# An HGRN2 attention block with a routed feed-forward: stores of x rows half a step later, the first slots' fetch two stages earlier, the first expert's transposes three stages later

## The chip, the cores and the metric

The kernel runs on one core of a Trainium2 chip, in one launch. The metric is the device time of that core in microseconds (us). TensorE (PE) does the matrix products and transposes; VectorE (DVE), ScalarE (ACT) and GpSimd (POOL) do elementwise work; SyncE (SP) only issues transfers (DMAs). GpSimd issues DMAs too, those that gather or scatter rows by a list. Each engine takes its instructions in the order in which the program lists them.

## What is computed

```python
# attention: q, k, v, f_logit are (4, 8, 768, 48)
f = 1.0 / (1.0 + np.exp(-f_logit))
for t in range(S):
    state = f[:, :, t, :, None] * state + np.einsum('bhd,bhe->bhde', k[:, :, t], v[:, :, t])
    y[:, :, t] = np.einsum('bhd,bhde->bhe', q[:, :, t], state)
x = y.transpose(0, 2, 1, 3).reshape(3072, 384)
# router: two of eight experts for each row
noisy = x @ w_gate + np.log1p(np.exp(x @ w_noise)) * noise
top2 = np.argpartition(-noisy, 2, axis=1)[:, :2]          # weights: softmax over the two
# experts: w1 is (8, 384, 1024), w2 is (8, 1024, 384)
out[mask] += top2_w[mask, k, None] * (np.maximum(x[mask] @ w1[e], 0.0) @ w2[e])
```

## The kernel before

**Attention in 24 pieces.** The sequence is cut into six chunks of 128 tokens, for each of four batch rows: 24 pieces, `n` = 0 to 23 (`NS`). For a piece there are seven stages: `forget` (transposes and log of the forget gate), `summed` (a running sum), `decays` (exponentials), `scaled` (transposes and scaling of q and k), `scores` (the 128 x 128 score blocks, L573, multiplied by the causal mask into `A`, L576), `output` (the y products, L591 and L602, and the new state) and `features` (L626: the x rows and the router's logits in one product; ACT copies the x rows to `xs`, L631). The main loop (L1292) runs steps `i`; in step `i` the stages are called in the fixed order forget, scaled, scores, summed, output, decays, features, each for the piece `i - lag` (lags in L1293). So in the last steps step 23 does sc 23, y 22 and xp 21, step 24 does y 23 and xp 22, and step 25 does xp 23. In the text "sc 23" stands for the scores of piece 23, and so on.

**What a stage has hung on it.** After a stage is called, the loop issues loads of later pieces on SP's queue (f after `forget`, q and k after `scaled`, v after `scores`), parts of the first experts' weights, clears of the output (`zeros`, L1253, 192 KB each), a step of the router's generator (`route`), at most one put of an entry into the expert lists (`put`, L703, a GpSimd DMA), a step of `first_loads`, and, once that has set `done["turned"]`, a piece of the expert work. One such round is what the change counts as a stage. The stores of x rows (`x_rows`, a tensor in the chip's main memory) are not issued where they are made: `features` puts them into the list `xw` (L632), and the loop takes them out.

**The expert work.** After half of the chunks are routed, the first 256 rows of the first four experts' lists are taken from the rows known so far. The 24 groups of 256 list entries are called pairs; the first four are items 0 to 3 (`NE` = 4). For each pair: `fetch` (L808) loads its list entries (`slots`) on SP, `gather` (L819) gathers the x rows by them with two GpSimd DMAs of 128 rows each, `turned` (L855) transposes the 128 rows on TensorE and DVE copies them to `xt_a`, `first_layer` (L907, four blocks of two: `hp`) does the first product with a ReLU on ACT, and `second_layer` (L1014) does the second product in seven products of half size (Strassen-Winograd), for which DVE makes sums of weights (`second_sums`, L879) and of hidden values (`inner_sums`, L996). The results are scattered with addition into the output (L1023). `ahead(1, k + NR + 1)` (L914) loads the first-layer weights of a later item into the buffer that the current one has just read for the last time.

**The seam.** `first_loads` is a generator that is stepped once a stage. It waits until the puts of the first half are issued, then some stages, and then goes through a written list of fetches, gathers and the first pair's two transposes with a number of stages to pause after each. Puts are held back between the first fetch and the first gather (L1332). The weights of pair 1 (`w1[1]` L834, `w2[1]` L837, in quarters) are loaded at the end of the loop. All this order is kept as traced on every engine (`in_order`, L1393). On SP's queue each DMA also waits for the eighth one before it, since their completion semaphores are taken in turn.

Of the kernel before, what the change touches and what calls it, by code (L numbers as in the profile page):

```python
# [331 lines left out]
def kernel(  # L332
# [157 lines left out]
    def load_router(part):  # L490

        if part < 2:
            for i, w in ((part, (moe_w_gate, moe_w_noise)[part]),):
                for odd in range(2):
                    for par in range(2):
                        nc.gpsimd.dma_start(out=w_rt[par * DP:par * DP + D, odd::2, XW + i * E:XW + (i + 1) * E],
                                          in_=w.rearrange("(a o r d) e -> o r d a e", o=2, r=2, d=D)[odd, par ^ odd])
        else:
            c = part - 2
            nc.sync.dma_start(out=noise[:, c], in_=moe_noise.rearrange("(b s) e -> s b e", b=B)[c * C:(c + 1) * C])  # L500
# [8 lines left out]
    xw, puts, n_put = [], [], []  # L509
# [8 lines left out]
    def load(nm, n):  # L518
        c, b = n // B, n % B
        if n < NCH * B:  # L520
            nc.sync.dma_start(out=pads[nm][n % RING[nm]][:, :, 0:D],
                              in_={"f": f_logit, "q": q, "k": k, "v": v}[nm][b, :, c * C:(c + 1) * C, :].rearrange("h t d -> t h d"))

    def clamp(n, engine=nc.gpsimd):
        if n < NCH * B:
            raw = pads["f"][n % RING["f"]][:, :, 0:D]
            engine.tensor_scalar(raw, raw, XMIN, None, ALU.max)
# [286 lines left out]
    def gather(p, halves=(0, 1)):  # L814

        if 0 in halves:
            xg[p] = moved.tile([128, 2, DM], F32, tag="xg", name=f"xg{p}", bufs=4)
        for s in halves:
            nc.gpsimd.indirect_dma_start(out=xg[p][:, s, :], out_offset=None, in_=x_rows[0:HALF * B * C] if p < NE else x_rows,  # L819
                                         in_offset=bass.IndirectOffsetOnAxis(ap=slots[p][:, s, 0:1], axis=0))  # L820
# [10 lines left out]
    def part_of_weights(k, which, part):  # L831
        if which == 1:
            few = slice(part * FF // 4, (part + 1) * FF // 4)
            nc.sync.dma_start(out=w1[k][:, :, few], in_=moe_w1[k].rearrange("(k p) f -> p k f", p=128)[:, :, few])  # L834
        else:
            few = slice(part * FO // 4, (part + 1) * FO // 4)
            nc.sync.dma_start(out=w2[k][:, few], in_=moe_w2[k].rearrange("(f p) d -> p f d", p=128)[:, few])  # L837
# [8 lines left out]
    def turned(p, s):  # L846
        k = item_of(p)
        if k < NE:
            to = xt_a[:, :, k % 2 * 256 + s * 128:k % 2 * 256 + (s + 1) * 128]
        else:  # L850
            side, at = columns(k)[p - first_of[k]][s]
            to = (wide[0] if side else xt_a)[:, :, at:at + 128]
        xp = one_bank(f"xgp{p}_{s}")
        for i in range(KO):
            nc.tensor.transpose(xp[:, i * 128:(i + 1) * 128], xg[p][:, s, i * 128:(i + 1) * 128], ident)  # L855
        (nc.vector.tensor_copy if p < NE else nc.scalar.copy)(to, xp[:, 0:DM].rearrange("d (k t) -> d k t", k=KO))
# [3 lines left out]
    def ahead(what, until):  # L860
        if what in (1, 2):
            most = len(items) if what == 1 else done[1]
        else:
            most = min(NP if len(n_put) == NCH * B * 2 else NE, NP if what == "fetch" else done["fetch"])
        while done[what] < min(until, most):
            t = done[what]
            done[what] += 1
            fetch(t) if what == "fetch" else gather(t) if what == "gather" else weights(t, what)
# [356 lines left out]
    first = len(nc.cur_bb.bb.instructions)  # L1225
# [5 lines left out]
    def warm_up(count):  # L1231
        for _ in range(count):
            nc.tensor.matmul(warm[:, 0:128], lhsT=ones, rhs=ones, start=True, stop=True)
# [24 lines left out]
    def first_loads():  # L1258
        while n_routed < HALF or len(n_put) < HALF * B * 2:
            yield  # L1260
        for _ in range(7):
            yield
        for what, p, pause in (("fetch", 1, 4), ("first", 0, 0), ("second", 0, 3), ("fetch", 2, 7), ("turned", 0, 0),
                               ("first", 1, 3), ("second", 1, 1), ("fetch", 3, 1)):
            if what == "fetch":
                ahead(what, p)
            elif what == "first":
                gather(p, (0,))
            elif what == "second":
                gather(p, (1,))  # L1270
                done["gather"] = p + 1
            else:
                for half in range(2):
                    turned(p, half)
                    yield
                done["turned"] = True
            for _ in range(pause):
                yield

    def tables():  # L1280
        for i, val in enumerate((0, 0, FAR, 0)):
            nc.gpsimd.memset(empty[:, :, i], val)
        nc.gpsimd.memset(entry, 0)
        for i, ids in ((0, row_of), (2, token)):
            nc.gpsimd.tensor_copy(entry[:, :, :, :, i], ids.unsqueeze(3).broadcast_to((128, NCH, B, 2)))
        nc.gpsimd.memset(zero, 0.0)
# [5 lines left out]
    for i in range(-3, NS + 2):  # L1292
        order = [(forget, -3), (scaled, -1), (scores, 0), (summed, -2), (output, 1), (decays, -2), (features, 2)]  # L1293
        if i < 0:
            order[0:2] = order[1::-1]
        for stage, lag in order:
            n = i - lag
            if not 0 <= n < NS:
                continue
            stage(n)  # L1300
            if stage is forget:
                load("f", n + 4)
                if n > 1:
                    clamp(n + 2)
                if n == 5:
                    tables()
            elif stage is scaled:
                for nm in "qk":
                    load(nm, n + 2) if n < 4 else load(nm, n + 3)
                    if n == 3:  # L1310
                        load(nm, n + 3)
                if n in (1, 2):
                    load_router(n - 1)
                while xw:
                    xw.pop(0)()
            elif stage is scores:
                for m in (n + 1,) if n < 4 else (2 * n - 3, 2 * n - 2) if n < 6 else (n + 3,):
                    load("v", m)
                if n in (2, 6, 7, 8, 9, 10):
                    load_router(2 + (2, 6, 7, 8, 9, 10).index(n))  # L1320
                elif n == 5:
                    nc.sync.dma_start(out=lists.rearrange("(p r) w -> p r w", p=128), in_=empty)
            elif stage is output:
                if 9 <= n < 17:
                    part_of_weights(0, 1 + (n - 9) // 4, (n - 9) % 4)
                elif n >= NS - 2:
                    part_of_weights(1, 1, 1 + (n - NS + 2) * 2)
            elif stage is features and n >= NS - 4:
                part_of_weights(1, 1, (n - NS + 4) * 2) if n < NS - 2 else zeros(4)
            next(router, None)  # L1330
            slot += 1
            if puts and slot % (2 if n_routed == HALF else 3) == 0 and not (done["fetch"] and not done["gather"]):  # L1332
                puts.pop(0)()
            next(first_pairs, None)

            if done["turned"] and (n_first < 5 or i >= NS - 3 and stage is not forget) and (n_first < 11 or i >= NS - 1):
                next(pieces)
                n_first += 1
        if i < 0:
            warm_up(4)  # L1340
        if i >= NS - 1:
            while xw:
                xw.pop(0)()
        n = i - 2
        if n >= 0 and n % B == B - 1:
            c = n // B
            router = chain(router, route(c))
            n_routed = c + 1
            if c == HALF - 1:
                router = chain(router, enough())  # L1350
                first_pairs = first_loads()
            if c == NCH - 1:
                router = chain(router, plan(), beyond())
# [19 lines left out]
    for item, piece in pieces:  # L1373
        p = first_of[item] + max(0, piece - 8) // 7 if item >= NE else item
# [58 lines left out]
```

## Time and profile before

| what | us |
|---|---|
| median of 3 runs | 655.39 |
| lowest, highest of them | 652.59, 659.07 |
| the profiled execution, its time | 659.87 |
| the profiled execution, its span | 658.1 |
| TensorE matmuls, busy | 637.8 |
| VectorE, ScalarE, GpSimd, busy | 442.8, 254.1, 270.2 |

The span is that from the first instruction to the last on the core. The mean granted TensorE clock is 0.987 of full speed. TensorE is busy in nearly all of the span, so the place to look is not a mean over the span but the few stretches in which it is not, and what ends them: the waits of TensorE, the chain of work that ended last, and the timelines of the engines that feed it. DMAs are read by the time at which they are issued and the time at which they land: over the whole run a store of x rows lands after 4.4 us (median), a fetch of slots after 7.7, a put into the lists after 6.1, a gather after 4.6, a clear of the output after 9.6, a whole weight load of 1.5 MB after 8.5.

### The profile page before, as it was taken

The numbers are of one execution on the slowest core, as the hardware profiler recorded it, in microseconds if no ns is written. First come the engines' busy times: TensorE is split into PE (matmuls) and PEld (weight loads), VectorE is DVE, ScalarE is ACT, GpSimd is POOL, SyncE is SP. The second block draws the span as 40 slices with busy tenths as digits, with TensorE's granted clock in tenths as the row PEclk, the third lists the DMA queues.
The fourth block names the chain that finished last, engine by engine and source line by source line (L and its number), as shares of the span: only waits on it lengthen the run. The fifth ranks groups of instructions, "written<-read, shape, count | busy, mean of one in ns | idle before, by whom it ended". The sixth has DMA issues, their size and how long they took to land.

```text
span 658.1 us, 12894 instructions
## 1 busy us (share of the span) xinstructions
PE 637.8 (97%) x4883; PEld 551.1 (84%) x4883; DVE 442.8 (67%) x993; ACT 254.1 (39%) x602; POOL 270.2 (41%) x301
## 2 busy tenths in 40 slices
PE   8999999979999999999999999999999999999991
PEld 8999999868989999989758965995698579899891
DVE  6777877954566577677657575666666666766751
ACT  6876776642222133233332233223332332232320
POOL 7743999743188521252501450334035114413021
PEclk9999999998999999999999999999999999999996
DMA  9999898774799323368707560925275247602112
GB/s 191 193 220 205 181 191 173 179 209 110 256 348 237 64 36 86 82 192 286 195 28 245 98 192 0 316 41 176 74 242 127 63 143 191 178 2 26 21 25 29
DMA packets 153897, 96.31 MB, mean 146 GB/s; under 512 B 115600, under 2 KB 146320, under 8 KB 153824
## 3 DMA queue, kind: packets, MB, share of 16 engines
q1 hardware_dynamic: 141648, 76.12, 42.0%
q0 software_dynamic: 12176, 19.25, 15.0%
q8 instruction: 41, 0.67, 0.4%
q14 instruction: 32, 0.26, 0.1%
HBM read 75.97 MB, written 19.62 MB: 145 GB/s over the span
## 4 chain that ended last, share of the span: by engine, by line
PE 90%; DMA 5%; SPq 1%; DVE 1%; POOL 1%; issue 0%; ACT 0%; POOLq 0%; DVEq 0%
PE y L1014 31%; PE P L932 8%; PE W L932 5%; PE Z L932 5%; PE V L932 5%; PE X L932 5%; PE hp L907 5%; PE sc L573 4%; PE y L591 4%; PE xp L626 3%; PE xgp L855 2%; PE y L602 2%; PE kp L533 1%; PE ds L597 1%; PE fp L533 1%; PE qp L533 1%
## 5 line engine op out<-in xcount | busy, mean ns | idle before, releaser
L1023 POOL DMA_INDIRECT out_dram<-ys,slots x48 | 80.3, 1672 | 150.0 <-ACT ys L1084 121.9
L1014 PE MATMUL y<-qk_all,f_all 128*128 128x192 f32 x576 | 105.3, 327 | 0.5 <-DVE f_all L996 0.5
L1014 PEld LDWEIGHTS y<-qk_all,f_all 128*128 128x128 f32 x576 | 93.3, 190 | 1.1 <-DVE f_all L996 1.1
L819 POOL DMA_INDIRECT xg<-x_rows,slots x48 | 52.9, 1102 | 50.8 <-DMA slots<-lists 35.0
L1014 PE MATMUL y<-w,hs_b 128*128 128x192 f32 x320 | 59.1, 328 | 0.0
L703 POOL DMA_INDIRECT lists<-entry,sloti x48 | 54.8, 1142 | 10.3 <-issue 9.5
L1014 PEld LDWEIGHTS y<-w,hs_b 128*128 128x128 f32 x320 | 52.9, 190 | 0.9
L1158 POOL DMA_INDIRECT out_dram<-ys_q,slots_q x5 | 8.6, 1720 | 104.4 <-DVE ys_q L1156 104.4
L907 PE MATMUL hp<-xt_a,w 128*128 128x256 f32 x192 | 43.4, 382 | 0.0
L968 ACT ACTIVATE hs_b<-hs_b 128x256 f32<-128x256 f32 (+1 forms) x32 | 15.1, 470 | 71.7 <-DVE hs_b L948 71.7
L907 PEld LDWEIGHTS hp<-xt_a,w 128*128 128x128 f32 x192 | 35.9, 190 | 4.9 <-issue 0.3
L932 PE MATMUL X<-xt_a,w 128*128 128x256 f32 (+1 forms) x128 | 39.7, 432 | 0.0
L932 PE MATMUL Z<-xt_b,v_all 128*128 128x256 f32 (+1 forms) x128 | 39.7, 432 | 0.0
L1073 DVE TENSOR_TENSOR ys<-P,y 128x192 f32<-128x192 f32 x24 | 8.5, 354 | 41.6 <-PE y L1014 25.6
L948 DVE TENSOR_TENSOR hs_b<-hs_a,X 128x256 f32<-128x256 f32 (+1 forms) x32 | 15.6, 487 | 29.9 <-PE X L932 29.7
L576 DVE TENSOR_TENSOR A<-sc,causal 128x1024 f32<-128x1024 f32 x24 | 29.3, 1221 | 8.9 <-PE sc L573 8.8
L1014 PE MATMUL y<-w,f_all 128*128 128x192 f32 x192 | 35.2, 326 | 0.0
L1084 ACT ACTIVATE ys<-ys,slots 128x384 f32<-128x384 f32 x23 | 14.1, 615 | 54.1 <-DVE ys L1080 54.1
L932 PEld LDWEIGHTS X<-xt_a,w 128*128 128x128 f32 x128 | 24.3, 190 | 10.1
L932 PEld LDWEIGHTS Z<-xt_b,v_all 128*128 128x128 f32 x128 | 24.3, 190 | 10.1
L948 DVE TENSOR_TENSOR hs_a<-hs_a,P 128x256 f32<-128x256 f32 (+1 forms) x64 | 31.1, 486 | 1.4
L1014 PEld LDWEIGHTS y<-w,f_all 128*128 128x128 f32 x192 | 31.8, 190 | 0.0
(200 smaller groups left out, 1442.2 us busy)
## 6 DMA issues: line engine op xcount, KB each, us to landing
w<-in_moe_w_dram SPq DMA_DIRECT2D x16, 1536.0 KB, 8.5
w_q<-in_moe_w_dram SPq DMA_DIRECT2D x10, 1536.0 KB, 10.3
w<-in_moe_w_dram SPq DMA_DIRECT2D x16, 384.0 KB, 6.1
f_all<-in_f_logit_dram SPq DMA_DIRECT2D x24, 192.0 KB, 3.7
qk_all<-in_q_dram SPq DMA_DIRECT2D x24, 192.0 KB, 4.9
qk_all<-in_k_dram SPq DMA_DIRECT2D x24, 192.0 KB, 4.9
v_all<-in_v_dram SPq DMA_DIRECT2D x24, 192.0 KB, 4.4
x_rows<-xs SPq DMA_DIRECT2D x24, 192.0 KB, 4.4
```

The costliest lines, as they stand in the source:

```text
L533: nc.tensor.transpose(p[:, cols(hp)], flat[:, cols(hp)], ident)
L573: nc.tensor.matmul(sc[:, par, cols(hp)], lhsT=kQ[n][rows(par), cols(hp)], rhs=qP[n][rows(par), cols(hp)], start=True, stop=True)
L576: nc.vector.tensor_tensor(A[n].rearrange("j r (a i) -> j (r a) i", i=C), sc.rearrange("j r (a i) -> j (r a) i", i=C), causal.unsqueeze(1). ...
L591: nc.tensor.matmul(at(hp, par), lhsT=vt[:, 2 * hp + par, :], rhs=A[n][:, par, cols(hp)], start=(hp < 2), stop=(c == 0 and hp >= HP - 2))
L626: nc.tensor.matmul(xp[:, hp, :], lhsT=yT[n][:, hp % 2, cols(hp // 2)], rhs=w_rt[:, hp, :], start=True, stop=True)
L703: into = nc.gpsimd.indirect_dma_start(out=lists, out_offset=bass.IndirectOffsetOnAxis(ap=sloti[:, r, b:b + 1], axis=0), in_=entry[:, c, b, ...
L819: nc.gpsimd.indirect_dma_start(out=xg[p][:, s, :], out_offset=None, in_=x_rows[0:HALF * B * C] if p < NE else x_rows, in_offset=bass.Indir ...
L907: nc.tensor.matmul(hp[:, o, :], lhsT=w1[home(k)][:, i, (fo + o) * 128:(fo + o + 1) * 128], rhs=xt_a[:, i, k % 2 * 256:(k % 2 + 1) * 256], ...
L932: nc.tensor.matmul(to, lhsT=x, rhs=y, start=start, stop=stop)
L948: nc.vector.tensor_tensor(to, x, y, ALU.add)
L1014: nc.tensor.matmul(P[name], lhsT=x[:, o, :], rhs=y[:, o, :], start=(o == 0), stop=(o == FH - 1))
L1023: into = nc.gpsimd.indirect_dma_start(out=out, out_offset=bass.IndirectOffsetOnAxis(ap=slots[p][:, s, 2:3], axis=0), in_=ys[s], in_offset= ...
```

## The change

`first_loads` steps five stages and not seven before the first fetch, and the list after it has the first pair's transposes behind the gathers of the second pair, with other pauses. Counted in stages after the puts of the first half, the first fetch goes from 7 to 5, the first gathers from 11 to 9, the second fetch from 14 to 12, the first pair's two transposes from 21 and 22 to 24 and 25, the second pair's two gathers from 23 and 26 to 17 and 18, and the third fetch from 27 to 26. The expert pieces start after the transposes, so they too start three stages later. The stores in `xw` are taken out after `output` and no longer after `scaled`, that is three stages later in the same step.

```diff
@@ first_loads
-        for _ in range(7):
+        for _ in range(5):
             yield
-        for what, p, pause in (("fetch", 1, 4), ("first", 0, 0), ("second", 0, 3), ("fetch", 2, 7), ("turned", 0, 0),
-                               ("first", 1, 3), ("second", 1, 1), ("fetch", 3, 1)):
+        for what, p, pause in (("fetch", 1, 4), ("first", 0, 0), ("second", 0, 3), ("fetch", 2, 5), ("first", 1, 1), ("second", 1, 6),
+                               ("turned", 0, 0), ("fetch", 3, 1)):
@@ main loop, after `scaled`
                 if n in (1, 2):
                     load_router(n - 1)
-                while xw:
-                    xw.pop(0)()
@@ main loop, after `output`
             elif stage is output:
+                while xw:
+                    xw.pop(0)()
                 if 9 <= n < 17:
                     part_of_weights(0, 1 + (n - 9) // 4, (n - 9) % 4)
```

In the list, `("fetch", p, ...)` loads the slots of all pairs below `p` that are not loaded yet, `("first", p, ...)` and `("second", p, ...)` are the two gathers of pair `p`, and `("turned", 0, 0)` is the two transposes of pair 0, a stage apart.

## The prediction

> **What bounds the kernel now.** I read the page's busy shares first: PE is busy 637.8 of 658.1 us, so only 20.3 us of the span are idle TensorE time. I split these with the waits view of PE and the timeline of its ends: 1.8 us at the start, 4.16 us in one wait near 142 us, 0.46 us in one near 190 us, and 13.9 us after the last matmul (it ends at 644.2). Elsewhere TensorE runs through: one attention step, as a sum of rows of the chain (0.44 fp, 0.44 qp, 0.44 kp, 0.44 kp turned, 1.09 sc, 1.02 y, 0.47 ds, 0.60 y, 1.07 xp), is 6.01 us, and steps follow each other every 6.0 us. The stage to price is the end of attention. First the waits of PE (total us, times, longest), then its timeline there (start us, us, line, op, and the idle time before):
>
> ```profile
> PE xgp L855 <- DMA xg<-x_rows,slots: 4.2, 1, 4.2
> ```
>
> ```profile
> 138.11 1.16 PE L573 MATMUL sc<-qP,kQ 64*128 64x128 f32 x16
> 139.20 1.09 PE L591 MATMUL y<-A,v_all 128*64 128x128 f32 x16
> 140.22 0.67 PE L602 MATMUL y<-qP,st 64*64 64x128 f32 x16
> 140.82 1.15 PE L626 MATMUL xp<-w_rt,yT 128*128 128x112 f32 x8
> 146.12 0.87 PE L855 MATMUL xgp<-ident,xg 128*128 128x128 f32 x3 [4.16 <-DMA xg<-x_rows,slots]
> 146.93 2.08 PE L573 MATMUL sc<-qP,kQ 64*128 64x128 f32 x16
> 148.94 0.90 PE L855 MATMUL xgp<-ident,xg 128*128 128x128 f32 x3
> ...
> 151.67 0.94 PE L602 MATMUL y<-qP,st 64*64 64x128 f32 x16
> ```
>
> The first expert's transposes wait for gathered rows, and the last scores (L573) stand behind them though their inputs were ready at 139.7. And after the wait the same scores take 2.08 us instead of 1.16. The windows view confirms a lower clock (stretch; length, PE, PEld, DVE, ACT, POOL busy; granted clock, DMA share, GB/s):
>
> ```profile
> 130.00:140.00 10.00, 10.00 (x152) 8.84 (x150) 9.11 (x16) 6.38 (x19) 1.35 (x2) 1.00 0.74 164
> 140.00:150.00 10.00, 5.84 (x54) 4.46 (x52) 3.04 (x7) 1.14 (x4) 8.15 (x12) 0.77 0.71 206
> 150.00:160.00 10.00, 10.00 (x85) 8.43 (x87) 5.21 (x19) 2.32 (x5) 3.81 (x7) 0.89 0.39 84
> ```
>
> Third, the SP queue's timeline, because it issues the fetch, the stores and the weights:
>
> ```profile
> 134.41 0.37 SPq L521 DMA_DIRECT2D v_all<-in_v_dram  x1
> 134.87 0.84 SPq L808 DMA_DIRECT2D slots<-lists  x1
> ...
> 142.77 14.65 SPq L632 DMA_DIRECT2D x_rows<-xs  x2
> 157.47 0.43 SPq L834 DMA_DIRECT2D w<-in_moe_w_dram  x1
> ...
> 176.70 2.34 SPq L837 DMA_DIRECT2D w<-in_moe_w_dram  x4
> ```
>
> The fetch leaves at 134.87 and lands 4.37 us later (chain of waits), the gather starts at 140.06 and lands 5.93 us later, at 145.99: that releases PE. A store of x rows held SP for 14.65 us (the stall delayed its input), and the second weights of pair 1 left only at 176.70, landing at 185.97; the sums that read them (L879) waited 6.67 us, which is the 0.46 us of PE at 190.
>
> **What the Trainium skill says.** "TensorE: Matmul & The Clock Gate", What's actually happening: the array falls to half clock after an idle window of about 3.4 us and needs about as long of work to recover, and the window is free-running, so this varies by run. The trace agrees: 4.16 us of idleness, then groups at up to 1.8 times their length until about 152. "DMA: Bandwidth & Descriptors", Anatomy of one DMA: a transfer costs about 2 us fixed, and waits for semaphores are held on the issuing sequencer. The 4 KB fetch took 4.37 us here, so the fixed part is larger under this load; SP's 14.65 us shows the second point.
>
> **The change, part by part.** The durations are of the profiled execution: 658.1 us of span, 659.87 as its time, 4.5 above the median 655.39 of the three runs.
>
> *Transposes three stages back.* Nothing is added: six transposes, two DVE copies (0.56 us) and all later pieces keep their number. By the built program's order PE now does sc 23, y 22, xp 21, first transposes, y 23, second transposes, xp 22, then the four hp blocks with xp 23 after the first. From xp's end at 141.96 at full speed: sc 1.09, y 1.02+0.60, xp 1.07 end at 145.74; there the first transposes need rows that in the trace before landed at 145.99, even with no earlier fetch. Wait left: 0.25 us at most, of 4.16. Next y 23 (its A: DVE 1.22 us after sc ends at 143.05, so 144.4; its v load needs to land before 146.1) ends at 147.69; the second transposes need the second gather, issued 1.34 us behind the first, so at 147.3 even unmoved. hp needs both copies: second transposes end 148.0, copy done about 148.7, and xp 22 covers until 149.1.
>
> *Clock.* Over the groups after the wait: xgp 0.87-0.49 and 0.90-0.49 (0.49: xgp at 170), sc 2.08-1.16, y 1.98-1.09, y 0.94-0.67: 0.38+0.41+0.92+0.89+0.27 = 2.87 us. Another way: from 146.12 to 170.10, 23.98 us, PE does work that sums to 21.2 (1.09+0.66+2 x 1.62+3 x 1.07+4 x 2.60+2 x 1.30), 2.8 us over. With a wait of 0.25 the clock doesn't fall: 2.8 us gone.
>
> *Fetch two stages forward.* One SP DMA of 4 KB moves ahead of the last v load and one store; it could leave at about 133.1 (k load ends 132.0, then v and a store at about 0.5 each). It must wait for the last put into the lists: issued at 126.07, landed by 134.87 at the latest, or the old fetch would have waited. So 0 to 1.7 us are gained; worth 0.25 us on PE, the rest is margin. What is queued behind a wait there is the last v load, no later than 135.3, with about 4.4 us to land, against 146.1: no cost. The next two fetches move up one and two SP places; pair 1's two gathers move ahead of two puts on POOL. PE needs pair 1 only at 170.1-6.9 = 163.2, and they are issued by about 148: cost nothing.
>
> *Stores half a step back.* 24 DMAs, same bytes. In attention a store then finds its input ready and v's load stands ahead of it; PE has no wait for loads there, so the gain is 0 and the bound of loss too: no load moves back except by one store's issue (0.3 to 0.7 us). At the end it matters: the held store's input now comes at about 147 and not 157, so SP passes the last part of pair 1's first weights at about 148, then 12 clears of the output, 3 stores or fetches and the second weights. The w1 load of item 2, which waits for PE's last hp and held SP until 166.81, is now behind these. Sixteen transfers ahead of the second weights, SP being at most eight ahead of landings (the program's waits), at 9.6 us median landing for a clear: at most two such rounds, so issued at the latest about 167, landed by 176; by bandwidth alone (16 x 192 KB and 1.5 MB at the 343 GB/s of 170 to 180 us) about 162. The sums need them by about 182.6-3.9 = 178.7. So the 0.46 us goes; item 2's w1, issued at 161 to 168 and landing in 8.5 us, is needed at 192.
>
> **Sum:** 4.16-(0 to 0.25) + 2.8 + 0.46 = 7.2 to 7.4 us. Profiled span 658.1 to 650.7; time 659.87 to 652.5.
>
> Against the median it is less sure. If the median run has the same stall, 655.39-7.4 = 648.0. But what can differ between runs of a program whose PE runs through? The stall hangs on two DMA latencies and on whether the clock falls; it can be all of the 4.5 us by which the profiled execution lies above the median (then 652.5 stays), and the fastest run, 652.59, is about what a run with no stall would give. I take the middle of 648.0 and 652.5: **650.0 us**.
>
> **Rivals.**
> (1) Forecast, 82%: the stall goes, 648.0 to 652.5, with about 1.5 us of scatter of a median either way.
> (2) A wait takes its place, 14%: the tail of attention loses its filler, for hp no longer lies between y and xp. If hp finds its copy late (0.3 us margin) or the second weights land at 180 to 183, 2 to 4 us of the gain are returned: 652 to 655. For it: SP's window and slow clears (9.6 us). Against it: 2.7 us of margin in the worst count.
> (3) Slower, 4%: the fetch holds SP for the last put, and the rows land late. Needed at 145.74; the change loses once they come over 4.2 us later than that, about 150, which means a fetch at 139, so a put landing 13 us after its issue at 126.07. The longest landing of a put in the trace is 10.8. The slow clock is then the same as before, so each us beyond costs one: rows at 155 would make it 655.39+5 = 660.
> (4) That the change doesn't act is excluded by the built order: both moves are there. That only the stores act is inside (2).
>
> **How the numbers follow.** A measurement of this kernel tells about 1% (the runs span 652.59 to 659.07). 1% faster is 648.84. Of case 1's 82%, 38 lie below it, 44 above, being centred just above; case 2's 14% is within; case 3's 4% is slower. The 80% range is case 1 with scatter, 646.5, up to the larger part of case 2, 654.5.
>
> **What would show it.** Right: no PE wait at L855 over 0.3 us; granted clock 1.00 in 140 to 160; sc 23 at 1.1 us at 142; the L837 transfers before 168; no L1014 wait on f_all; the end of PE near 637. Wrong: a PE wait at L855 or L907 over 1 us, a slow clock after it, or a wait at L1014 for sums on late weights. If all these signs are right and the time is above 653, the stall of the profiled execution was not that of usual runs.

## The result and the profile after

| | kernel before | changed kernel |
|---|---|---|
| median of 20 runs each, us | 655.25 | 652.08 |
| lowest to highest, us | 651.47 to 660.1 | 651.48 to 654.07 |
| runs over 655 us | 11 of 20 | 0 of 20 |
| profiled execution: time, span, us | 659.87, 658.1 | 652.09, 650.3 |

The ratio is 0.9948 with a 95% interval of 0.9924 to 0.9972: 0.5% faster. The profiled executions differ by 7.8 us, the medians by 3.2.

The place that the prediction was about, in the timeline of TensorE of the changed kernel (start us, us, line, op; an idle time before an instruction would stand at its end):

```profile
141.07 1.15 PE L626 MATMUL xp<-w_rt,yT 128*128 128x112 f32 x8
142.14 1.16 PE L573 MATMUL sc<-qP,kQ 64*128 64x128 f32 x16
143.23 1.09 PE L591 MATMUL y<-A,v_all 128*64 128x128 f32 x16
144.26 0.67 PE L602 MATMUL y<-qP,st 64*64 64x128 f32 x16
144.85 1.15 PE L626 MATMUL xp<-w_rt,yT 128*128 128x112 f32 x8
145.84 0.49 PE L855 MATMUL xgp<-ident,xg 128*128 128x128 f32 x3
146.26 1.09 PE L591 MATMUL y<-A,v_all 128*64 128x128 f32 x16
147.28 0.67 PE L602 MATMUL y<-qP,st 64*64 64x128 f32 x16
147.88 0.55 PE L855 MATMUL xgp<-ident,xg 128*128 128x128 f32 x3
```

No bracket: the transposes (L855) find their rows. The last scores (L573) run at 142.14, four groups ahead of them, in 1.16 us and not in 2.08. The rows were gathered from 135.06 on here, 5.0 us earlier than in the execution profiled before, so this profile alone doesn't say whether the later place was needed; experiments 2, 5 and 7 look at that. The windows view has the same (stretch; length, PE, PEld, DVE, ACT, POOL busy; granted clock, DMA share, GB/s):

```profile
140.00:150.00 10.00, 10.00 (x140) 8.48 (x137) 6.15 (x25) 3.52 (x11) 6.34 (x12) 1.00 0.82 231
150.00:160.00 10.00, 10.00 (x52) 8.92 (x51) 5.30 (x13) 2.46 (x6) 3.81 (x5) 1.00 1.05 360
```

TensorE is busy throughout at full clock, and the DMA engines, at 0.39 of their time in the second stretch before, are now full in it. Why is seen in SP's timeline:

```profile
131.86 0.37 SPq L808 DMA_DIRECT2D slots<-lists  x1
...
146.80 0.34 SPq L632 DMA_DIRECT2D x_rows<-xs  x1
147.18 0.43 SPq L834 DMA_DIRECT2D w<-in_moe_w_dram  x1
147.66 2.30 SPq L1253 DMA_DIRECT2D out_dram<-zero  x4
...
156.39 2.08 SPq L837 DMA_DIRECT2D w<-in_moe_w_dram  x4
```

The fetch leaves 3.0 us earlier than in the execution profiled before (131.86 for 134.87), no store holds SP for 14.65 us, and the second weights of pair 1 leave at 156.39 for 176.70. The waits view of PE for the whole kernel has two waits left, both in the first 14 us:

```profile
PE warm L1233 <- DVE ones L443: 1.1, 1, 1.1
PE fp L533 <- POOL f_all L527: 0.4, 1, 0.4
```

### The profile page after: what moved, and what is told of

It is laid out like the page before. It is cut to its first block, busy times and chain, and to the rows that moved or that the text cites. A ratio compares the mean times of both kernels' runs of the same rounds, so it can differ in the third digit from the quotient of the medians.

```text
span 650.3 us, 12900 instructions
## 1 busy us (share of the span) xinstructions
PE 634.9 (98%) x4883; PEld 549.6 (85%) x4883; DVE 443.4 (68%) x993; ACT 253.9 (39%) x602; POOL 270.4 (42%) x301
## 4 chain that ended last, share of the span: by engine, by line
PE 95%; POOL 1%; DMA 1%; SPq 0%; DVE 0%; issue 0%; POOLq 0%
PE y L1014 33%; PE P L932 8%; PE hp L907 6%; PE W L932 5%; PE Z L932 5%; PE V L932 5%; PE X L932 5%; PE xp L626 4%; PE sc L573 4%; PE y L591 4%; PE xgp L855 2%; PE y L602 2%; PE kp L533 2%; PE qp L533 1%; PE ds L597 1%; PE fp L533 1%
## 5 line engine op out<-in xcount | busy, mean ns | idle before, releaser
L1014 PE MATMUL y<-qk_all,f_all 128*128 128x192 f32 x576 | 105.3, 327 | 0.0
L1014 PEld LDWEIGHTS y<-qk_all,f_all 128*128 128x128 f32 x576 | 93.3, 190 | 0.4 <-DVE f_all L996 0.4
L1014 PE MATMUL y<-w,hs_b 128*128 128x192 f32 x320 | 59.1, 328 | 0.0
L1014 PEld LDWEIGHTS y<-w,hs_b 128*128 128x128 f32 x320 | 52.9, 190 | 0.9
L1014 PE MATMUL y<-w,f_all 128*128 128x192 f32 x192 | 35.2, 327 | 0.0
L1014 PEld LDWEIGHTS y<-w,f_all 128*128 128x128 f32 x192 | 31.8, 190 | 0.0
```

The lines of the kernel that those rows point to most:

```text
L1014: nc.tensor.matmul(P[name], lhsT=x[:, o, :], rhs=y[:, o, :], start=(o == 0), stop=(o == FH - 1))
```

## The experiments

The runs of the kernel before stood in two groups, and the profiled execution was of the long one. So the first question was whether the stall is in some executions only; the second, which of the three parts removes it. Theory A: the transposes' wait for rows, with the slow clock after it, is the whole loss, and their new place removes it. Rival B: the stores' place does. Rival C: the earlier fetch does. Rival D: the long executions have another cause.

**1. The kernel before, unchanged (e0).**

> The kernel before, unchanged, for the clock and span of each of its executions. Theory A (the loss is the wait of the first transposes for gathered rows plus the slow clock that follows, and it is there in some executions only): the times fall into two groups, 651.5 to 654 and 657 to 660, the long ones with a mean granted clock near 0.987 as in the profiled one and the short ones near 0.993 as in the changed kernel. Rival D (the spread comes from the start or from the last scatters, and the stall is in every execution): the clock is the same, 0.987, in long and short executions.

Of 22 executions 19 took 651.7 to 654.0 us with mean clocks of 0.991 to 0.994, and three took 659.4 to 660.7 with 0.987 and 0.988. Of the 75 executions of the same kernel that ran beside it 36 were over 655, all with clocks of 0.986 to 0.991, and those below 654 had a median of 652.36. That fits theory A and not D: nearly all long executions are those with the slow clock. This profile caught a short one (TensorE, then two lines of SP):

```profile
142.12 0.49 PE L855 MATMUL xgp<-ident,xg 128*128 128x128 f32 x3
142.54 1.16 PE L573 MATMUL sc<-qP,kQ 64*128 64x128 f32 x16
...
132.63 0.72 SPq L808 DMA_DIRECT2D slots<-lists  x1
...
170.09 2.11 SPq L837 DMA_DIRECT2D w<-in_moe_w_dram  x4
```

The same kernel, the same order of instructions, and no bracket at the transposes. Its fetch left at 132.63 and its first gather started at 136.55, against 134.87 and 140.06 in the long execution. The second weights leave late here too, at 170.09, and a wait of 0.4 us at L1014 is there as well: that small loss is not part of the stall. The median of the kernel before is thus a matter of how many of its executions stall, and that share isn't steady: 3 of 22 here, 36 of 75 beside it. As a control this run also says what a ratio is worth: 0.9975 (0.9946 to 1.0004) for one kernel against itself.

**2. The transposes alone three stages later (e1).**

```diff
-        for what, p, pause in (("fetch", 1, 4), ("first", 0, 0), ("second", 0, 3), ("fetch", 2, 7), ("turned", 0, 0),
-                               ("first", 1, 3), ("second", 1, 1), ("fetch", 3, 1)):
+        for what, p, pause in (("fetch", 1, 4), ("first", 0, 0), ("second", 0, 3), ("fetch", 2, 9), ("first", 1, 1),
+                               ("turned", 0, 0), ("second", 1, 1), ("fetch", 3, 1)):
```

> Only the first transposes moved back three stages; first fetch at 7 stages and stores of x rows as before. Theory A: TensorE reaches the transposes at about 145.8 and the rows land at about 146, so a wait of 0 to 0.5 us is left, no slow clock; median 652 to 652.5, all of the gain. Rival B (the stores' place on SP carries the gain) and rival C (the earlier fetch carries it): at least half of the gain is missing, median 653.5 or more, wait of 1 us or more at the transposes.

Median 651.99, ratio 0.9947 (0.9923 to 0.997), one of 22 over 655, at 655.06. That is as much as the whole change won, with this part alone:

```profile
145.89 0.49 PE L855 MATMUL xgp<-ident,xg 128*128 128x128 f32 x3
...
157.22 2.03 SPq L837 DMA_DIRECT2D w<-in_moe_w_dram  x4
```

The transposes don't wait. But the first gather started at 135.38 here and landed 3.8 us later, at about 139.2, in time for the old place (about 142) too. And one long execution of 22 is not clearly fewer than the three of the control. Whether the place helps when the rows are late is tried in 5 and 7. The early second weights, at 157.22, come with this part alone.

**3. The stores alone half a step later (e2).**

```diff
             elif stage is scaled:
...
-                while xw:
-                    xw.pop(0)()
...
             elif stage is output:
+                while xw:
+                    xw.pop(0)()
```

> Only the stores of x rows moved back half a step; fetch and transposes as before. Theory A: the transposes still wait, the fetch leaves at most 1 us earlier, median 654 to 656 with the two groups of before. Rival B: median 652 to 652.5, no wait, one group.

Median 652.72, ratio 0.9981 (0.9955 to 1.0007); 6 of 22 over 655, up to 657.7. The median is lower than expected, but stalls are left, so rival B falls as the whole cause. The profiled execution was a short one, its fetch leaving at 132.50, and its second weights leave no earlier than in e0's:

```profile
170.14 2.17 SPq L837 DMA_DIRECT2D w<-in_moe_w_dram  x4
```

**4. The fetch alone two stages earlier (e3).**

```diff
-        for _ in range(7):
+        for _ in range(5):
...
-("fetch", 2, 7), ("turned", 0, 0),
+("fetch", 2, 9), ("turned", 0, 0),
```

> Only the first fetch and gather moved forward two stages; transposes and stores as before. Theory A with the estimate of 0 to 1.7 us earlier rows: the wait is 2.5 to 4 us in the profile, and [...]the median lies between, 652.5 to 655. Rival C: no wait, median 652 to 652.5. Rival B: no change, 655 to 656.

Median 652.64, ratio 0.9958 (0.9931 to 0.9985); two of 22 over 655, at 656.3 and 659.1. No wait in its profile, where 2.5 to 4 us were expected: a miss, since the expectation took the long execution for the usual one. The fetch left at 133.95, later than in e0's short execution. Rival C falls in its strict form (long executions are left). Against the control's 3 of 22, neither 6 nor 2 nor the 1 of e1 says for sure what a part does to the share.

**5. Late rows in every execution (e6).** Since chance shares can't be compared, the next three kernels make the rows late always: the first fetch goes behind the store whose input comes at 139.4. The puts are held until the first gather, so that the lists aren't written under the fetch.

```diff
-        for _ in range(7):
+        for _ in range(18):
             yield
-        for what, p, pause in (("fetch", 1, 4), ("first", 0, 0), ("second", 0, 3), ("fetch", 2, 7), ("turned", 0, 0),
+        for what, p, pause in (("fetch", 1, 2), ("first", 0, 0), ("second", 0, 1), ("turned", 0, 0), ("fetch", 2, 0),
...
-... and not (done["fetch"] and not done["gather"]):
+... and not (len(n_put) >= HALF * B * 2 and not done["gather"]):
```

> The kernel before with the rows made late in every execution: its first fetch at 18 stages and not 7, behind the store whose input comes at 139.4, and the puts held until the first gather. Fetch at about 139.8; rows about 8.5 us later, 148.3 (3.1 to 4.4 of fetch, 0.8, 3.6 to 5.9 of gather); TensorE is there at 142.1. Theory A: a wait of 5 to 8 us and 2.5 to 3 us of slow clock in every execution, one group, 652.4+8 to 11 = 660 to 663, mean clock 0.985 to 0.987. Rival D (long executions have another cause): the two groups stay, the short one below 655.

Median 661.06, all 20 between 659.8 and 662.2, clocks 0.984 to 0.989: one group, and it is the long one.

```profile
140.96 1.15 PE L626 MATMUL xp<-w_rt,yT 128*128 128x112 f32 x8
147.88 0.88 PE L855 MATMUL xgp<-ident,xg 128*128 128x128 f32 x3 [5.78 <-DMA xg<-x_rows,slots]
148.69 2.08 PE L573 MATMUL sc<-qP,kQ 64*128 64x128 f32 x16
150.70 0.90 PE L855 MATMUL xgp<-ident,xg 128*128 128x128 f32 x3
151.53 1.15 PE L591 MATMUL y<-A,v_all 128*64 128x128 f32 x16
```

The price can be added up from these lines: 5.78 of wait, and 0.39+0.92+0.41+0.06 = 1.8 us by which the four groups exceed 0.49, 1.16, 0.49 and 1.09. With the 652.4 of a short execution this makes 660.0. The profiled execution itself took 659.81; the median of the 20 is 661.06.

**6. Late rows, with work on TensorE in the wait (e7).** As e6, with 36 matmuls of ones ahead of the transposes. It adds work and leaves out none.

```diff
             else:
+                idle = one_bank("idle")
+                for _ in range(36):
+                    nc.tensor.matmul(idle[:, 0:128], lhsT=ones, rhs=ones, start=True, stop=True)
                 for half in range(2):
                     turned(p, half)
```

> The same late rows, with 36 matmuls of ones (about 4 us) on TensorE ahead of the first transposes, so that its wait falls to 2 to 3.5 us of idleness. Work is added, none left out. Theory A with the clock as an effect of idleness: the rows land at the same time, but the scores after them take 1.1 us and not 2.1; 2 to 3 us faster than the run with late rows alone, mean clock about 0.992. If the slow matmuls after the wait come from the rows or their transfers and not from idleness: no faster than with late rows alone.

Median 661.13, the same as without the work; clocks 0.991 to 0.994. The filling was twice as long as estimated:

```profile
142.34 8.22 PE L1274 MATMUL idle<-ones 128*128 128x128 f32 x72
150.39 0.49 PE L855 MATMUL xgp<-ident,xg 128*128 128x128 f32 x3
150.81 1.16 PE L573 MATMUL sc<-qP,kQ 64*128 64x128 f32 x16
```

It holds TensorE for 8.05 us (to the next group), 2.3 us beyond the wait of 5.78, and yet nothing is lost, because the scores after it take 1.16 and not 2.08. The first gather was issued at 143.11, as late as in e6 (142.91). So the slow matmuls are an effect of idleness and not of the rows: 1.8 us by the sum above, about 2.2 by the two medians (8.05-5.78, less the 0.07 between them). That it would be faster was a miss, by the size of the filling.

**7. Late rows, with the transposes three stages later (e8).** The list of e6 with `("second", 0, 4)` for `("second", 0, 1)`.

> The same late rows (fetch at 18 stages), with the first transposes three stages later as in the changed kernel, stores as before. Theory A: TensorE reaches them at 145.8 and waits 2 to 4 us, about 3.8 us less than with late rows alone; the clock falls in few executions or none; 655 to 658. It is still slower than the kernel before in its short executions: the rival of the prediction on the slower side, a late fetch. If the transposes' place were worth nothing by itself: 660 to 663 like the run with late rows alone.

Median 657.47, all 20 between 655.1 and 659.7, below all 20 of e6 (659.8 to 662.2). The transposes' place is worth 3.6 us where the rows are always late:

```profile
145.31 1.15 PE L626 MATMUL xp<-w_rt,yT 128*128 128x112 f32 x8
149.72 0.84 PE L855 MATMUL xgp<-ident,xg 128*128 128x128 f32 x3 [3.27 <-DMA xg<-x_rows,slots]
150.49 1.98 PE L591 MATMUL y<-A,v_all 128*64 128x128 f32 x16
152.39 1.02 PE L602 MATMUL y<-qP,st 64*64 64x128 f32 x16
```

The wait is 3.27 for 5.78. But the clock fell after a wait of 3.27 us too (1.98 for 1.09, 1.02 for 0.67), in nearly all executions (clocks of 0.987 to 0.992), where few were expected. 652.4+3.27+0.35+0.89+0.35 = 657.3; the profiled execution took 657.15. And this kernel has the changed kernel's order on TensorE and is still slower than the kernel before, 1.003 (1.0001 to 1.0058): the place alone wins nothing against rows that come late enough.

**8. A shorter filling (e9), the kernel before, the stores alone and the fetch alone again.** These four ran together, on another chip.

> The late rows with 20 matmuls of ones ahead of the first transposes and not 36. In the run with 36 they took 8.05 us (0.22 us each, twice the estimate), 2.3 us longer than the wait of 5.8 us, and yet the time was the same. With 20 they take 4.5 us, about 1.3 us of idleness is left. Theory A with the clock as an effect of idleness: no slow clock, 661.1-2.5 = 658 to 659, mean clock 0.992 or more. If the 36 had hidden nothing of the clock and the two equal times were chance: 661.

> The kernel before again, since 3 of 22 executions were long (over 655) in its first run and 36 of 75 beside it. If the share of long executions is a property of the kernel: near 45%, 10 of 22, in which case the first 3 were chance or a matter of that load. If it differs from load to load: any share, and shares of single runs can't be compared.

> Stores alone moved, again. 6 of 22 were over 655 in its first run. Theory A (the stores only give the fetch a little margin): 5 to 10 of 22 over 655, in the short executions 652 to 653.5. Rival B: none over 655.

> Fetch alone moved, again. 2 of 22 were over 655 in its first run. Theory A with a margin of 0 to 1.7 us from the fetch: some long executions left, 1 to 6 of 22, fewer than with the stores alone. Rival C: none over 655.

On this chip the kernel before took 665.97 us (65 runs) and none of its executions was below 661. TensorE now waits for loads inside attention as well; in the waits of PE of the kernel before, run again:

```profile
PE xgp L855 <- DMA xg<-x_rows,slots: 5.7, 1, 5.7
PE kp L533 <- DMA qk_all<-in_k_dram: 1.7, 2, 0.9
```

Medians and ratios: before again 666.38 (0.9988, 0.9967 to 1.0009), stores alone 663.08 (0.9956, 0.9931 to 0.9981, 12 runs), fetch alone 665.2 (0.9982, 0.9961 to 1.0003), short filling 665.89 (0.9988, 0.9965 to 1.001). The expectations in us don't hold here, and the medians don't answer the question of the filling. The profile of the short filling does bear on it:

```profile
142.24 0.63 PE L533 MATMUL qp<-ident,qk_all 128*128 128x128 f32 x4 [1.88 <-DMA qk_all<-in_q_dram]
...
144.79 1.97 PE L591 MATMUL y<-A,v_all 128*64 128x128 f32 x16
...
158.95 0.52 PE L855 MATMUL xgp<-ident,xg 128*128 128x128 f32 x3 [1.14 <-DMA xg<-x_rows,slots]
159.40 1.16 PE L573 MATMUL sc<-qP,kQ 64*128 64x128 f32 x16
```

After the filling a wait of 1.14 us was left, and the scores ran at full speed, as expected. Earlier, a wait of only 1.88 us for a load was followed by y products of 1.97 us for 1.09.

The share of stalls, then, isn't the kernel's own. The stores alone were faster here, but not shown to be so by earlier rows: in the two profiles the fetch left at the same time (140.96, and 140.94 in the kernel before). The wait at L855 was 2.5 us for 5.7 because TensorE came there 1.35 us later (the product ahead of the transposes started at 145.71 for 144.36) and the first gather, from its start to the transposes, took 3.9 us for 6.5. Why the stores alone helped wasn't tried.

**9. The changed kernel again (e10).**

> The changed kernel again, beside the kernel before, on whatever chip it lands. In the last four runs the loads of q and k landed late (TensorE waited 0.9 to 3.6 us for them inside attention, and the kernel before took 666 us, with a wait of 5.7 us at the transposes). Theory A (the gain is what the wait and its slow clock cost on that chip): beside a kernel before of 653 to 656 a ratio of 0.994 to 0.998; beside one near 666 a ratio of 0.985 to 0.992, since the wait is there in every execution. If the gain had to do with neither: the same ratio 0.995 on both.

Again another chip, with the kernel before at 667.12: the changed kernel took 664.44, ratio 0.9941 (0.9921 to 0.9962). A miss: the gain is no larger there than on a quick chip, 2.7 us for the 5 to 10 expected. The same ratio on both was named beforehand as the sign that the gain has to do with neither the wait nor the clock. The transposes don't wait in the profile. TensorE is held up elsewhere, and the clock falls (the last line is of the windows view, where 0.70 is the granted clock):

```profile
144.13 0.95 PE L573 MATMUL sc<-qP,kQ 64*128 64x128 f32 x9
145.91 0.50 PE L573 MATMUL sc<-qP,kQ 64*128 64x128 f32 x4 [0.83 <-issue]
147.34 0.49 PE L573 MATMUL sc<-qP,kQ 64*128 64x128 f32 x3 [0.93 <-DMA w<-in_moe_w_dram]
...
148.77 0.45 PE L591 MATMUL y<-A,v_all 128*64 128x128 f32 x3 [0.68 <-issue]
...
150.00:160.00 10.00, 9.22 (x85) 7.42 (x86) 5.02 (x24) 3.06 (x9) 0.39 (x2) 0.70 0.49 149
```

Gaps inside the last scores and the y products, between matmuls of one group; "issue" is time for which the profile shows no wait. DVE stood still for 8.2 us in the same stretch. From the xp product at 143.06 to the transposes at 155.61 TensorE took 12.55 us, for 4.77 in the first profile of the changed kernel (141.07 to 145.84): 7.8 us were lost in the same stretch, as much as by the stall, to something else. That instructions arrived late would fit, but it was not tested: what this is stays open, as does whether the kernel before has it on that chip. So on that chip the gain is measured, and its cause is not shown.

## Why the prediction was right, point by point

- **Bound and stall.** Right. The wait of 4.16 us at L855, the slow clock after it and the 0.46 us at L1014 are gone, and TensorE ends 7.7 us earlier: its last matmul started at 642.81 and ran 1.46, now at 635.14. That late rows cost a wait and a slow clock is shown by e6 and e7, that the new place takes 3.6 us off by e6 and e8. That the place, and not rows that came early by themselves, kept all 20 executions of the changed kernel below 655 is argued from this, and not shown for each.
- **The sum for the profiled execution.** 7.2 to 7.4 us were forecast, 7.8 measured: 652.5 predicted, 652.09 found. Transposes were to start at 145.74 (145.84), hp to wait for nothing (it doesn't), the second weights to leave before 168 (156.39). The prediction put these early weights under the stores' new place; e1 has them at 157.22 and e2 at 170.14, so they come with the transposes.
- **The fetch.** It was to be 0 to 1.7 us earlier; it is 3.0 us earlier than in that execution, but only 0.8 us earlier than in a short execution of the same kernel before (132.63), so most of the 3.0 us is a difference between executions and not shown to be the change's.
- **From that execution to the median.** Here the forecast was 650.0, the middle of 648.0 and 652.5, because it was open whether the median run had the same stall. It did not: the kernel before has short executions near 652.4 and long ones near 659, and its median of 655.25 lies between. The term mis-sized is the gain against the median: 5.4 us taken (655.39 to 650.0), 3.2 measured, because about half of the executions had nothing to gain. The end of the bracket that took a run without the stall to be at 652.5 was the right one; the lower end, 648.0, was met by no run. The range 646.5 to 654.5 holds 652.08, and within 1% had the larger chance.
- **Clock.** The Trainium skill's idle window of about 3.4 us, in "TensorE: Matmul & The Clock Gate", What's actually happening, is not borne out as a lower limit here. The clock fell in e8 after an idle time of 3.27 us, and on the chip of experiment 8 after waits of 2.46 us (stores alone) and 1.88 us (e9), the y products taking 1.97 us for 1.09 both times. It did not fall after 1.14 us (e9). So a wait of 2 to 3 us, had one been left, would not have been safe. The slow groups lasted about 3.7 us in e6 (147.88 to 151.6), near what the page gives for the recovery, but 6.4 us in the kernel before (146.12 to 152.54).
- **Rivals.** No wait took the place of the one removed. The slower side was not met, but its mechanism is real: with the fetch at about 140, e8 is slower than the kernel before. The point named, rows landing near 150, was named against a stalled kernel before; against its short executions it's the first wait that counts, and e8's rows came at 149.7.

## What to carry to other kernels

Ask of a stall whether it is in every execution before pricing it: here one profile showed 7.8 us and the median gained 3.2. A spread of 1% in a kernel whose busiest engine is busy 97% of the time came here from a transfer that arrives sometimes just in time and sometimes not. Where you see such a spread, look at the times and mean clocks of many runs, and for a trial make the transfer late always. On an engine that takes its instructions in order, put work that waits for nothing ahead of an instruction that waits for a DMA: moving six transposes behind 3.7 us of such work took 3.6 us off where the rows were always late.

## What the runs showed that was not expected

One kernel's share of executions over 655 us was 3 of 22 and 36 of 75 on one chip and 22 of 55 on a second, and on two other chips the same kernel took 666 and 667 us. The slow clock followed waits of 3.27, 2.46 and 1.88 us too; where its price was added up it was 1.6 to 2.9 us.
